# Where q, k and the tails of each batch are turned: crossbar, whole-array or half-array transposes, in a sliding-window attention with a channel mix behind it

## The chip, the cores and the metric

The kernel runs on one core of one Trainium2 chip. The metric is device time in microseconds of one execution; lower is better. A core has TensorE (PE: matmuls, and transposes as matmuls with an identity), VectorE (DVE), ScalarE (ACT), GpSimd (POOL, here an issuer of DMAs that cast fp32 to bf16), SyncE (SP, an issuer of DMAs and of the DMA crossbar's transposes) and 16 DMA engines that all queues share.

## The reference

Eight batches of eight heads, 576 positions, head size 64. Attention looks back over a window of 128 with a linear penalty per head; its output, heads side by side, is the input of a channel mix.

```python
scores = scale * np.matmul(q, k.transpose(0, 1, 3, 2))
rel = pos[:, None] - pos[None, :]
bias = slopes[:, None, None] * (-np.abs(rel))[None]        # slopes = 2 ** -(h + 1)
scores = np.where((rel >= 0) & (rel < 128), scores + bias[None], -1e9)
attn = softmax(scores)                                     # over keys
x = matmul(attn, v).transpose(0, 2, 1, 3).reshape(8, 576, 512)
# channel mix; x_prev is x one position earlier
xk = mu_k * x + (1 - mu_k) * x_prev
xr = mu_r * x + (1 - mu_r) * x_prev
k = np.maximum(xk @ w_k, 0)                                # 512 -> 1024
out = sigmoid(xr @ w_r) * ((k * k) @ w_v)                  # 1024 -> 512
```

## The kernel before

**An order planned on the host.** Each step (a block of matmuls, a copy, a DMA issue) is a node with an estimated length, dependences, the buffers that it takes and frees, and a priority. `Plan.run` plays the nodes through in an event loop and emits the instructions of each engine in the order that comes out; on the chip each engine runs its own list in order, with semaphores between them. `rank` gives an attention step of batch b and head pair g (k = 4b + g) the turn `(k - A[e]) * SLOPE` on engine e; a step of the channel mix has as its turn the sum of the estimated matmul times of the mix before it. The smaller turn goes first when both are ready. `LOADS` is the order of the first loads on POOL's queue: v and V are the two halves of batch 0's v, 2 and 3 the second part of its q and k (heads 0 to 3, 4 to 7), t its tails, K and k the halves of w_k, a, b and c batch 1's q and k, tails and v, R is w_r, W and w are the halves of w_v. Batches 2 to 7 follow as a, b, c.

**Attention, per batch and pair of heads (g = 0 to 3).** q and k are loaded with positions on the partitions and have to be turned so that the head dimension lies there (two heads of 64 rows). The first 512 positions are turned in one of three ways. Batch 0 is special: loaded in two parts, `part` 0 from fp32 stages (L1046, L1049) and `part` 1 by `qk_quad`. `WIDE` batches are loaded head by head with four successive positions in one piece, and are turned by `qk_quad` (L1002: 64x64 blocks). `XB` batches are turned by the DMA crossbar from SP's queue, eight transposes per batch (L467, `flip`). The others are turned by `qk_full`: eight 128x128 transposes into one PSUM bank, one ACT copy of 1024 columns. With `QM` above 0, `qk_some` does it for QM pairs at a time, in 64-row halves: two transposes run in the two halves of the array, into two banks, and four ACT copies of 512 columns (for QM = 2) follow. The last 64 positions (the tails) come as one tile for q and k and are turned by four PE transposes and a DVE copy (`tails`, L856), or for batches in `XTT` by one crossbar transpose (`tail_flip`, L560).

`scores` (L658, K = 64 rows) fills two PSUM pairs, ACT takes exp (L672), DVE multiplies by the mask (L685; batch 0 adds the bias by matmuls, L645, instead). `attend` (L716) multiplies by v with a column of ones behind it, and DVE divides (L722, L727). The output is turned back: by the crossbar for batches in `XO` (6 and 7, L839), otherwise on PE, either whole (`out_t`, L754: five 128x128 transposes, one ACT copy of 576) or, with `OM` above 0, in 64-row halves (`out_some`, L771: ten half-array transposes, two banks, two ACT copies). `shift` makes xk and xr on DVE (L814, L821).

**The channel mix** goes over pairs of batches P, in column ranges of 256, 512 or 384: w_k (L907), relu on ACT (L914), square (L880), then per 128 rows w_r (L925), tanh on ACT (L932), w_v (L941), a product on DVE (L946) and the output's DMA. `order` counts these ranges.

**Buffers.** Four single PSUM banks (`uno`, class p1) are shared by the mix, the transposes and the warm-up matmuls; two pairs (`duo`, p2) serve scores and attend. There are two buffers each for the loaded q and k (cb), v (vs), tails (ts), and crossbar results (qx), and four for turned q and k (qk). Ninety warm-up matmuls (L619) have the last priority and fill PE's free time at the start.

Of the kernel before, what the change touches and what calls it, by code (L numbers as in the profile page):

```python
# [179 lines left out]
def kernel(  # L180
# [12 lines left out]
    nc = tc.nc  # L193

    B, H, S, D = q.shape
    DM = H * D
    DF = moe_w_k.shape[1]
    G = H // 2
    NF = S // 128
# [7 lines left out]
    SM = 128 * NF  # L207
    RELU_SCALE = 0.5 ** 0.5

    PE, ACT, DVE, POOL, SPE, FAB, VIR = "PE", "ACT", "DVE", "POOL", "SP", "FAB", "VIR"  # L210
    NQ, NA, NX, NV, NC = 4, 4, 3, 2, 2
    XB = range(5, B)
    XO = range(6, B)
    X0 = 16
    NWARM = 90
    LOADS = 'v23KtVkabcRWw'
    XD = 6
    OTL = 1.5
    FIN = 384
    RATE = 284.0  # L220
    WIDE = (1,)
    PART_WIDE = True
    QUAD = 0.0565
    RUN = {2: 64 * 284 / 329.0, NF: 128 * 284 / 357.0}
    FLIP = 1.25
    NO = 5
    WAIT = 2.0
    QM = 0
    OM = 1

    def XU(b, g):
        return (DVE,)

    def SQ(order):
        return (DVE,)

    XT0 = (ACT,)
    QK0 = (ACT, DVE)
# [1 line left out]
    FT = (2, 3)  # L240
    KQ = ACT
    VCUT = True
    XTT = range(6, B)
    MMASK = False
    VDEP = 1
    TCOST = 1.5
# [14 lines left out]
    ts_buf = many(2, [128, H, D], BF16, "ts")  # L261
    tt_buf = many(2, [128, G, 3, 64], BF16, "tt")
# [23 lines left out]
    ident = cst.tile([128, 128], BF16, name="ident")  # L286
# [16 lines left out]
    def one(h):  # L303
        return uno[h.idx if h.cls == "p1" else N1 + h.idx]

    def two(h):
        return duo[h.idx]

    plan = Plan(dict(qx=2, xb=2, p2=2, p1=N1, pt=4 - N1, qk=NQ, at=NA, xu=NX, vs=NV, cb=NC, ts=2, tt=2, xt=2, dl=2, dl0=4,
                     xk=2, rl=3, kk=3, rs=4, ot=NO),  # L310
                {}, WAIT)
# [5 lines left out]
    def act_t(n, sb=False):  # L317
        return (n + (112 if sb else 61)) / 1200.0

    def dve_t(n, fast=1):  # L320
        return (n / fast + 66) / 960.0

    AHEAD = 30.0
    A = {PE: 14.25, ACT: 4.00, DVE: 4.50, VIR: 0}
    NBIAS = 4
    XRL = 3.0
    MODE = 0
    EARLY = 0.0
    SLOPE = 4.5

    def rank(prio):

# [9 lines left out]
    def op(e, dur, deps, prio, emit, need=(), free=()):  # L342
        prio = rank(prio)
        return plan.add(e, dur, LAT.get(e, 0.2) if isinstance(e, str) else LAT[e[0]] if len(e) == 1 else 0.22,
                        deps, prio, emit, need, free)

    last = {}

    def virtual(key, holds):
        n = plan.add(VIR, 0.0001, 0.0001, [last.get(key)], (0,), None, holds)  # L350
        last[key] = n
        return n
# [11 lines left out]
    def dma(queue, kb, issue, emit, deps=(), need=(), free=(), lat=(1.0, 0.9)):  # L364
        n = plan.add(queue, issue, 0.0, list(deps) + [last.get(queue)],
                     (len(plan.nodes),), emit, need)
        last[queue] = n
        return fab(queue, kb / RATE, n, lat, free)
# [38 lines left out]
    n_ident = dve_op(0.11, emit_ident, [n_iota], (0, -1))  # L407
# [21 lines left out]
    def issue_t(nd):  # L429
        return 0.53 + 0.00034 * nd  # L430
# [16 lines left out]
    def tail_load(b):  # L447
        h = Hold("ts")
        g = virtual("ts", [h])
        ns = []  # L450
        for i in range(2):
            src = (q, k)[i][b, :, SM:S].rearrange("h p d -> p h d")
            ns.append(dma(POOL, 128 * TCOST, issue_t(512), lambda e, i=i, src=src: nc.gpsimd.dma_start(
                out=ts_buf[h.idx][64 * i:64 * i + 64], in_=src), [g]))
        return h, ns
# [4 lines left out]
    def full_load(b, i, h, g):  # L460
        src = (q, k)[i][b, :, 0:SM].rearrange(
            "h (r p) d -> p h r d" if b in XB else "h (p r) d -> p h r d", p=128)
        return [dma(POOL, 256, issue_t(1024), lambda e, r=r: nc.gpsimd.dma_start(  # L463
# [58 lines left out]
    th, tl, n_w, src1 = {}, {}, {}, {}  # L522
# [31 lines left out]
    cw, ch, cl, xbh, xbl, tth, ttl, ttg = {}, {}, {}, {}, {}, {}, {}, {}  # L554
# [10 lines left out]
    def batch_load(b, what):  # L565
# [7 lines left out]
        elif what == "b":  # L573
            th[b], tl[b] = tail_load(b)
            if b in XB:
                xbh[b] = Hold("qx")
# [9 lines left out]

    for what in LOADS:
        load_step(what)
# [8 lines left out]
    for (c0, n) in DSEG:  # L597
        n_copy[c0] = dve_op(dve_t(n, 4), lambda e, c0=c0, n=n: nc.vector.tensor_copy(
            out=dist[:, c0:c0 + n], in_=dist[:, 0:n]), [n_dist], (0, 1))
    n_sid = [dve_op(0.1, lambda e, h=h: nc.vector.tensor_scalar(  # L600
        out=sid[:, h], in0=ident, scalar1=-(2.0 ** (-(h + 1))) / scale, scalar2=None,
# [6 lines left out]
    def emit_mu(e):  # L608
# [5 lines left out]
        out=mu_sb.rearrange("p i o -> p (i o)"), in_=one(h_mu)[:, 0:2 * NPO]), (), [h_mu])  # L614
# [12 lines left out]
    def copy_any(e, out, in_):  # L627
        (nc.scalar.copy if e == ACT else nc.vector.tensor_copy)(out=out, in_=in_)  # L628
# [213 lines left out]
            res.append(fab(SPE, 1.0 * rows / 128, n, (1.0, 0.9), [hx]))  # L842
        return res

    def tails(b, prio):
        htt = Hold("tt")
        hs = th[b]
        if b in XTT:
            plan.follow(last["tt"], ttg[b])
            last["tt"] = ttg[b]  # L850
            return tth[b], ttl[b]
        hp = Hold("p1")

        def emit(e):
            for g in range(G):
                nc.tensor.transpose(  # L856
                    one(hp).bitcast(BF16)[:, 128 * g:128 * g + 128],
                    ts_buf[hs.idx][:, 2 * g:2 * g + 2].rearrange("p h d -> p (h d)"), ident)

        def emit_c(e):  # L860
            copy_any(e, tt_buf[htt.idx][:, :, 0:2].rearrange("p g t c -> p g (t c)"),
                     one(hp).bitcast(BF16)[:, 0:128 * G].rearrange("p (g w) -> p g w", g=G))

        t = op(PE, 0.0565 * G, list(tl[b]) + [n_ident], prio + (0,), emit, [hp], [hs])
        g = virtual("tt", [htt])
        c = [op(DVE, dve_t(512), [t, g], prio + (0,), emit_c, (), [hp])]
        return htt, c


# [2 lines left out]

    n_hw = 39 + sum(4 if g in FT else 2 for g in range(3)) + 8 * len(XB) + len(XTT) + NJ * len(XO)
    n_split = -n_hw % 8
# [119 lines left out]
    def qk_quad(b, g, nr, buf, deps, prio, c0, hq, take, free):  # L994

        hp = [Hold("p1"), Hold("p1")]

        def emit(e):
            for n in range(2 * nr):
                for hl, r in ((0, 0), (1, 1), (1, 0), (0, 1)):  # L1000
                    rows = slice(64 * r, 64 * r + 64)
                    nc.tensor.transpose(  # L1002
                        one(hp[r]).bitcast(BF16)[64 * hl:64 * hl + 64, 64 * n:64 * n + 64],
                        buf()[rows, n // nr, 2 * g + hl, n % nr], ident[rows, rows])

        t = op(PE, QUAD * 2 * nr, list(deps) + [n_ident], prio + (3,), emit,
               hp + ([hq] if take else []), free)
        t.rows, t.lazy = (64, 64), True
        w = 64 * nr
        ys = [op(QK0 if b == 0 else ACT, {ACT: act_t(2 * w), DVE: dve_t(2 * w)}, [t], prio + (3,),  # L1010
                 lambda e, r=r: copy_any(
            e, qk_buf[hq.idx][:, :, c0 + w * r:c0 + w * r + w].rearrange("p t (c r) -> p t c r", r=nr),
            one(hp[r]).bitcast(BF16)[:, 0:2 * w].rearrange("p (t r c) -> p t c r", t=2, r=nr)),
                 (), [hp[r]]) for r in range(2)]
        return hq, ys
# [6 lines left out]
    for part in range(2):  # L1022
        if part == 1:
            htt, n_tt = tails(0, (0, 0, 1, 0))
        for g in range(G):
            prio = (0, 0, part, g)
# [12 lines left out]
            hp = Hold("p1") if part == 0 else None  # L1039
# [13 lines left out]
            if part:  # L1053
                ys = qk_quad(0, g, 2, lambda: part_buf, cs, prio, 256, hq0[g], False, [])[1]
            else:
                cold = 1.8 if part == 0 and g < 2 else 1.0
                t = op(PE, (0.115 if f32 else 0.0565) * 4 * cold, cs + [n_ident], prio + (3,), emit_t,
                       [hp] + ([hq0[g]] if part == 0 else []))
                ys = [op(QK0, {ACT: act_t(512), DVE: dve_t(512)}, [t], prio + (3,),
                       lambda e, part=part, g=g, hp=hp, f32=f32: copy_any(  # L1060
                    e, qk_buf[hq0[g].idx][:, :, 0:256],
                    one(hp).rearrange("p (t c) -> p t c", t=2)) if f32 else copy_any(
                    e, qk_buf[hq0[g].idx][:, :, 256 * part:256 * part + 256].rearrange(
                        "p t (c r) -> p t c r", r=2),
                    one(hp).bitcast(BF16)[:, 0:512].rearrange("p (t r c) -> p t c r", t=2, r=2)),
                    (), [hp])]
            ha = Hold("at")
            es = []
            for j, (pieces, m0) in enumerate(PART[part]):
# [8 lines left out]
            r, hx = attend(0, g, t0, t1, ha, es + vl[0][0:2] + (vl[0][2:] + blank if part else []),  # L1078
                           prio)
            a, c = out_t(0, g, t0, t1, hx, [r], prio, xh[0], xth[0], late if part == 0 else None)  # L1080
# [31 lines left out]
    for j, (c0, n) in enumerate(MSEG):  # L1112
        n_mcopy.append(op(DVE, dve_t(8 * n, 4), ms + n_mcopy, (2, j),
                          lambda e, c0=c0, n=n: nc.vector.tensor_copy(
            out=mask[:, 0:H, c0:c0 + n], in_=mask[:, 0:H, 0:n])))
# [48 lines left out]
    for b in range(1, B):  # L1164
# [6 lines left out]
        htt, n_tt = tails(b, (0, b, 0, 0))  # L1171
        for g in range(G):
            prio = (0, b, 0, g)
            ha = Hold("at")
            if b in XB:
                hq, y = xbh[b], xbl[b]
# [13 lines left out]
            r, hx = attend(b, g, 0, NJ, ha, [m0, m1] + vl[b] + rs[0:1], prio)  # L1190
# [60 lines left out]
```

The softmax here doesn't subtract the row's maximum and nothing guards it: scores larger than these inputs give would overflow.

## Time and profile before

| | |
|---|---|
| median of 4 runs | 235.41 us (234.73 to 236.2) |
| profiled execution | 236.2 us, its span 234.1 us |
| clock granted to TensorE | 1.00 |
| PE, DVE, ACT, POOL busy | 227.4, 189.4, 160.8, 97.6 us |
| DMA: POOL's queue | 102736 packets, 16.26 MB |
| DMA: SP's and ACT's queues | 26592 packets, 14.50 MB |
| crossbar transposes | 24 of q and k, 10 of outputs, 2 of tails |

The profile is one execution. Busy times overlap between engines. Matmuls are pipelined, so the time shown for one is longer than its share of PE: the distance from start to start tells what a block costs. "L907" is a line of the kernel, and instructions of a helper all have the helper's line; where a wait is listed, the name behind the arrow is what ended it.

### The profile page before, as it was taken

How to read it: one execution, taken by the hardware profiler on the slowest of the kernel's cores; microseconds unless marked ns; L12 is line 12 of the kernel's file. 1: busy time of each engine (PE TensorE's matmuls, PEld its weight loads, DVE VectorE, ACT ScalarE, POOL GpSimd, SP SyncE). 2: the span in 40 equal slices, each digit the busy share in tenths (PEclk: the TensorE clock that was granted, in tenths of full speed). 3: DMA queues.
4: the chain of work that ended last, by engine and by line, in shares of the span. 5: the costliest groups of instructions: out<-in, count | busy, mean ns of one | idle time of the engine just before them, and what ended most of it. 6: DMA issues, size and time to landing. Idle time of an engine off the chain costs nothing.

```text
span 234.1 us, 6268 instructions
## 1 busy us (share of the span) xinstructions
PE 227.4 (97%) x2487; PEld 136.9 (58%) x2487; DVE 189.4 (81%) x427; ACT 160.8 (69%) x292; POOL 97.6 (42%) x124
## 2 busy tenths in 40 slices
PE   7999988999999999999999999999999999999994
PEld 6576866456575765555565755454655744445462
DVE  6577977987897999989989979995869996974242
ACT  3478999659998987984884975947594726326251
POOL 8976673897892694057807854200000000000000
PEclk9999999999999999999999999999999999999999
DMA  6999999999999799679999999996242124121122
GB/s 162 176 174 195 164 174 180 148 201 194 168 137 172 86 143 187 121 108 173 202 137 144 140 186 187 162 111 170 79 101 89 48 48 146 46 90 48 60 74 90
DMA packets 131100, 31.73 MB, mean 136 GB/s; under 512 B 120056, under 2 KB 127232, under 8 KB 131072
## 3 DMA queue, kind: packets, MB, share of 16 engines
q0 software_dynamic: 102736, 16.26, 101.5%
q1 hardware_dynamic: 26592, 14.50, 27.9%
q10 hardware_dynamic: 1744, 0.59, 1.0%
q8 instruction: 19, 0.31, 0.6%
q14 instruction: 9, 0.07, 0.1%
HBM read 33.56 MB, written 9.44 MB: 184 GB/s over the span
## 4 chain that ended last, share of the span: by engine, by line
PE 89%; ACT 5%; DMA 2%; issue 1%; DVE 1%; SPq 0%; DVEq 0%; ACTq 0%
PE uno L941 27%; PE uno L907 26%; PE uno L925 14%; PE duo L716 6%; PE duo L658 6%; PE uno L771 2%; PE uno L1154 2%; ACT at L672 2%; DMA qx<-in_q_dram 2%; PE duo L645 1%; PE uno L619 1%; ACT mask L1088 1%; ACT qk L628 1%; PE uno L1046 1%; PE uno L856 1%
## 5 line engine op out<-in xcount | busy, mean ns | idle before, releaser
L941 PE MATMUL uno<-wv_sb,kk 128*128 128x512 bf16 (+2 forms) x296 | 71.8, 374 | 0.0
L907 PE MATMUL uno<-xk,wk_sb 128*128 128x256 bf16 (+2 forms) x416 | 69.5, 314 | 0.7 <-ACT rl L914 0.4
L672 ACT ACTIVATE at<-duo 128x1024 bf16<-128x1024 f32 (+2 forms) x68 | 65.9, 1005 | 5.8 <-PE duo L658 5.3
L914 ACT ACTIVATE rl<-uno 128x256 bf16<-128x256 f32 (+2 forms) x104 | 47.3, 493 | 20.3 <-PE uno L907 19.1
L907 PEld LDWEIGHTS <-wk_sb 128*128 128x128 bf16 x416 | 38.7, 98 | 22.1 <-issue 0.9
L685 DVE TENSOR_TENSOR at<-at,mask 128x1024 bf16<-128x1024 bf16 x56 | 37.7, 680 | 8.1 <-ACT at L672 7.8
L438 POOL DMA_DIRECT2D vs<-in_v_dram x32 | 28.3, 899 | 33.9 <-PE duo L716 30.4
L941 PEld LDWEIGHTS <-kk 128*128 128x128 bf16 x296 | 26.4, 98 | 26.2
L880 DVE TENSOR_TENSOR kk<-rl 128x256 bf16<-128x256 bf16 (+2 forms) x104 | 33.0, 336 | 9.3 <-ACT rl L914 7.8
L932 ACT ACTIVATE rs<-uno 128x512 bf16<-128x512 f32 x36 | 22.2, 615 | 26.1 <-PE uno L925 23.1
L925 PE MATMUL uno<-wr_sb,xr 128*128 128x512 bf16 x144 | 37.0, 379 | 0.5 <-ACT rl L914 0.5
L946 DVE SCALAR_TENSOR_TENSOR ot<-rs,uno 128x512 f32<-128x512 bf16 (+2 forms) x37 | 24.7, 669 | 12.1 <-PE uno L941 9.7
L821 DVE SCALAR_TENSOR_TENSOR xk<-dl,mu_sb,xt 128x576 bf16<-128x576 bf16 (+1 forms) x32 | 24.8, 781 | 0.4
L716 PEld LDWEIGHTS <-at 128*128 128x128 bf16 x576 | 21.8, 98 | 5.7 <-issue 0.6
L821 DVE SCALAR_TENSOR_TENSOR xr<-dl,mu_sb,xt 128x576 bf16<-128x576 bf16 (+1 forms) x32 | 24.5, 771 | 0.0
L463 POOL DMA_DIRECT2D cb<-in_k_dram x24 | 21.3, 906 | 7.4 <-DMA wv_sb<-in_moe_w_v_dram 3.4
L628 ACT COPY xt<-uno 128x256 bf16<-128x256 bf16 (+1 forms) x48 | 17.1, 405 | 9.0 <-PE uno L771 8.8
L463 POOL DMA_DIRECT2D cb<-in_q_dram x24 | 21.3, 925 | 2.0 <-DMA vs<-in_v_dram 2.0
L925 PEld LDWEIGHTS <-xr 128*128 128x128 bf16 x144 | 13.5, 98 | 14.6 <-issue 0.7
L628 ACT COPY qk<-uno 128x1024 bf16<-128x1024 bf16 (+2 forms) x26 | 18.9, 778 | 3.0 <-PE uno L1049 1.7
L716 PE MATMUL duo<-vs,at 128*128 128x65 bf16 x448 | 19.1, 193 | 0.0
L814 DVE TENSOR_TENSOR dl<-xt 128x576 bf16<-128x576 bf16 (+1 forms) x32 | 13.8, 436 | 4.2 <-ACT xt L628 4.2
(78 smaller groups left out, 209.5 us busy)
## 6 DMA issues: line engine op xcount, KB each, us to landing
out_dram<-ot SPq DMA_DIRECT2D x30, 256.0 KB, 5.1
vs<-in_v_dram POOLq DMA_DIRECT2D x32, 128.0 KB, 7.2
cb<-in_q_dram POOLq DMA_DIRECT2D x24, 128.0 KB, 7.6
cb<-in_k_dram POOLq DMA_DIRECT2D x24, 128.0 KB, 7.5
out_dram<-ot SPq DMA_DIRECT2D x10, 128.0 KB, 1.8
wk_sb<-in_moe_w_k_dram POOLq DMA_DIRECT2D x2, 512.0 KB, 8.3
wv_sb<-in_moe_w_v_dram POOLq DMA_DIRECT2D x2, 512.0 KB, 10.9
qx<-in_k_dram ACTq DMA_DIRECT2D x4, 128.0 KB, 4.8
```

Source lines behind the costliest of these rows:

```text
L438: return dma(POOL, 256, issue_t(1024), lambda e: nc.gpsimd.dma_start(out=vs_buf[h.idx][:, j, :, 0:D], in_=v[b, :, 128 * j:128 * j + 128].r ...
L463: return [dma(POOL, 256, issue_t(1024), lambda e, r=r: nc.gpsimd.dma_start(out=cb_buf[h.idx][:, i, r], in_=src[:, :, r]), [g]) for r in ra ...
L628: (nc.scalar.copy if e == ACT else nc.vector.tensor_copy)(out=out, in_=in_)
L672: lambda e, ah=ah, w=w, hp=hp: nc.scalar.activation(out=ah(), in_=two(hp)[:, :, 0:w], func=AF.Exp, scale=float(scale)), (), [hp])
L685: nc.vector.tensor_tensor(out=a, in0=a, in1=m, op=ALU.mult)
L716: nc.tensor.matmul(a[:, hl, t - t0], lhsT=at[:, lo:lo + 128], rhs=vs[:, u, 2 * g + hl, :] if u < NF else tvb[:, 2 * g + hl], start=(u == u ...
L821: lambda e: nc.vector.scalar_tensor_tensor(out=buf[hk.idx][:, g, e0 + c0:e0 + c1], in0=dls(), scalar=mu[:, g:g + 1], in1=xc(1), op0=ALU.mu ...
L880: nc.vector.tensor_tensor(out=out, in0=in_, in1=in_, op=ALU.mult)
L907: nc.tensor.matmul(one(hp)[:, 0:n], lhsT=wk_sb[:, po, 128 * fo:128 * fo + 128], rhs=xk_buf[hx.idx][:, po, c0:c1], start=(po == 0), stop=(p ...
L914: a = op(ACT, act_t(n), [s], pr, lambda e, hp=hp, hr=hr: nc.scalar.activation(out=rl_buf[hr.idx][:, 0:n], in_=one(hp)[:, 0:n], func=AF.Rel ...
L925: nc.tensor.matmul(one(hp), lhsT=xr_buf[hx.idx][:, po, 128 * c:128 * c + 128], rhs=wr_sb[:, po], start=(po == 0), stop=(po == NPO - 1))
L941: nc.tensor.matmul(one(hv)[:, a:b], lhsT=kk_buf[hk.idx][:, fo, o:o + 128], rhs=wv_sb[:, fo, a:b], start=(fo == 0), stop=(fo == NFO - 1))
```

## The change

Batch 5's q and k leave the crossbar (`XB` from batch 6). Batches 3, 4 and 5 are turned by `qk_some` in pairs of g (`QM` 2), batch 2 joins batch 1 in the head-by-head form (`WIDE`), and the copies of batches 1 and 2 may go to ACT or DVE (`QK1`). Tails of batches 4 and 5 go to the crossbar (`XTT` from 4); batch 0's tails are loaded with four positions in a piece and turned by 16 small matmuls and two DVE copies (`TW`). Outputs of batches 1 to 5 are turned whole, not in halves (`OM` 0). The squares of mix orders 0 to 2 may go to ACT. w_k's first half is loaded before batch 0's second part of q and k, and w_r before batch 1's v. The planner's constants (lengths of quads and runs, turns, wait for 64-row work) change too.

```diff
-    XB = range(5, B)
+    XB = range(6, B)
-    LOADS = 'v23KtVkabcRWw'
-    XD = 6
+    LOADS = 'vK23tVkabRcWw'
+    XD = 4
-    WIDE = (1,)
+    WIDE = (1, 2)
-    QUAD = 0.0565
-    RUN = {2: 64 * 284 / 329.0, NF: 128 * 284 / 357.0}
+    QK1 = (ACT, DVE)
+    TW = (0,)
+    QUAD = 0.040
+    RUN = {2: 64 * 284 / 345.0, NF: 128 * 284 / 390.0}
-    WAIT = 2.0
-    QM = 0
-    OM = 1
+    WAIT = 1.0
+    QM = 2
+    OM = 0
     def SQ(order):
-        return (DVE,)
+        return (DVE, ACT) if order < 3 else (DVE,)
-    XTT = range(6, B)
+    XTT = range(4, B)
-    A = {PE: 14.25, ACT: 4.00, DVE: 4.50, VIR: 0}
+    A = {PE: 7.75, ACT: 4.50, DVE: 4.00, VIR: 0}
-    XRL = 3.0
+    XRL = 4.0
-    SLOPE = 4.5
+    SLOPE = 4.7
@@ tail_load
+        if b in TW:
+            for i in range(2):
+                ns.append(dma(POOL, 104, issue_t(128), lambda e, i=i: nc.gpsimd.dma_start(
+                    out=ts_buf[h.idx].rearrange("p h d -> p (h d)")[:, 256 * i:256 * i + 256],
+                    in_=(q, k)[i][b, :, SM:S].rearrange("h (c r) d -> h c (r d)", r=4)), [g]))
+            return h, ns
@@ tails (the code before is now tails_full, for b not in TW)
+            for n in range(8):
+                for hl in range(2):
+                    nc.tensor.matmul(
+                        one(hp)[64 * hl:64 * hl + 64, 64 * n:64 * n + 64],
+                        lhsT=ts_buf[hs.idx][:, n],
+                        rhs=ident.rearrange("p (g t c) -> p t g c", g=G, t=2)[:, hl],
+                        start=True, stop=True)
+        t = op(PE, 0.03 * 16, list(tl[b]) + [n_ident], prio + (0,), emit, [hp], [hs])
+        c = [op(DVE, dve_t(256), [t, g], prio + (0,), lambda e, i=i: copy_any(
+            e, tt_buf[htt.idx][:, :, i].rearrange("p g (c r) -> p g c r", r=4),
+            one(hp)[:, 256 * i:256 * i + 256].rearrange("p (r g c) -> p g c r", r=4, g=G)),
+                (), [hp]) for i in range(2)]
@@ qk_quad
-        ys = [op(QK0 if b == 0 else ACT, {ACT: act_t(2 * w), DVE: dve_t(2 * w)}, [t], prio + (3,),
+        ys = [op(QK0 if b == 0 else QK1, {ACT: act_t(2 * w), DVE: dve_t(2 * w)}, [t], prio + (3,),
```

More of the change, by code (lines that the diff above doesn't have):

```diff
@@ L843, in out_flip, with tails_full @@
         return res
[L845 to L851, printed above, removed]
+    def tails_full(b, prio, htt, hs):
         hp = Hold("p1")
@@ L866, in tails, with emit @@
         c = [op(DVE, dve_t(512), [t, g], prio + (0,), emit_c, (), [hp])]
+        return htt, c
+    def tails(b, prio):
+        htt = Hold("tt")
+        hs = th[b]
+        if b in XTT:
+            plan.follow(last["tt"], ttg[b])
+            last["tt"] = ttg[b]
+            return tth[b], ttl[b]
+        if b not in TW:
+            return tails_full(b, prio, htt, hs)
+        hp = Hold("p1")
+        def emit(e):
+            for n in range(8):
[6 more added lines that the diff above has]
+        t = op(PE, 0.03 * 16, list(tl[b]) + [n_ident], prio + (0,), emit, [hp], [hs])
+        g = virtual("tt", [htt])
+        c = [op(DVE, dve_t(256), [t, g], prio + (0,), lambda e, i=i: copy_any(
+            e, tt_buf[htt.idx][:, :, i].rearrange("p g (c r) -> p g c r", r=4),
+            one(hp)[:, 256 * i:256 * i + 256].rearrange("p (r g c) -> p g c r", r=4, g=G)),
+                (), [hp]) for i in range(2)]
         return htt, c
```

## The prediction

> **What bounds the kernel now.** I read the page first, its busy times and the chain that ended last:
>
> ```profile
> ## 1 busy us (share of the span) xinstructions
> PE 227.4 (97%) x2487; PEld 136.9 (58%) x2487; DVE 189.4 (81%) x427; ACT 160.8 (69%) x292; POOL 97.6 (42%) x124
> ...
> PE 89%; ACT 5%; DMA 2%; issue 1%; DVE 1%; SPq 0%; DVEq 0%; ACTq 0%
> ```
>
> TensorE (PE) carries the end. But "busy" counts the warm-up matmuls of L619, which compute nothing and are planned only where PE has nothing else. So I read busy time by stretches (columns after the stretch: its length, then busy us and count for PE, weight load, DVE, ACT, POOL):
>
> ```profile
> 0.00:10.00 10.00, 8.49 (x60) 6.07 (x61) 5.93 (x37) 4.07 (x5) 8.40 (x17) 1.00 1.21 166
> 10.00:20.00 10.00, 10.00 (x189) 6.92 (x188) 8.06 (x26) 7.01 (x15) 7.46 (x11) 1.00 1.73 181
> 20.00:30.00 10.00, 9.60 (x198) 7.41 (x197) 8.62 (x27) 9.73 (x28) 7.12 (x9) 1.00 2.10 171
> 30.00:40.00 10.00, 8.62 (x166) 6.51 (x165) 7.64 (x20) 9.73 (x20) 5.32 (x7) 1.00 1.62 185
> 40.00:50.00 10.00, 10.00 (x116) 5.51 (x115) 9.71 (x19) 6.42 (x11) 8.84 (x11) 1.00 2.22 164
> ```
>
> From 40 us on PE never idles; from 20 to 40 us it does, and there ACT is full (9.73 of 10). Next, PE's own waits from 43 to 231 us, and POOL's longest over the run:
>
> ```profile
> PE uno L907 <- ACT qk L628: 0.2, 1, 0.2
> ```
> ```profile
> POOL vs L438 <- PE duo L716: 30.4, 4, 11.7
> ```
>
> PE waits 0.2 us in 188, so there the time is the sum of PE's work. POOL stands idle 30 us until PE's attention frees a buffer: from 74 us on loads are early, not late. Last, PE in order of time (start, busy, then what). A block's real cost is the next block's start minus its own:
>
> ```profile
> 23.78 0.45 PE L619 MATMUL uno<-warm 128*128 128x128 bf16 x5
> ...
> 29.51 1.00 PE L1002 MATMUL uno<-ident,cb 64*64 64x64 bf16 x64
> 30.68 0.27 PE L856 MATMUL uno<-ident,ts 128*128 128x128 bf16 x2 [0.17 <-ACT qk L628]
> 31.40 0.27 PE L856 MATMUL uno<-ident,ts 128*128 128x128 bf16 x2 [0.45 <-issue]
> 31.51 1.47 PE L907 MATMUL uno<-xk,wk_sb 128*128 128x256 bf16 x12
> 32.91 0.56 PE L658 MATMUL duo<-qk 64*128 64x256 bf16 x8
> ...
> 33.46 0.45 PE L1002 MATMUL uno<-ident,cb 64*64 64x64 bf16 x32
> 33.84 1.05 PE L907 MATMUL uno<-xk,wk_sb 128*128 128x256 bf16 x8
> ...
> 38.49 1.02 PE L925 MATMUL uno<-wr_sb,xr 128*128 128x512 bf16 x4 [0.48 <-ACT rl L914]
> ```
>
> **PE time lost at the start.** Warm-up blocks, start to next start: 0.27, 0.45, 0.22, 0.68, 0.12, 0.28, 0.67 from 10 to 18 us, 2.69 in all; 0.29 and 0.45 at 23.78 and 24.84. From 26 to 38.5 us blocks are stretched against the same block unhindered: L1002 x32 takes 0.80 at 26.18 and 0.38 at 33.46 (+0.42); the x64 at 29.51 1.17 against 0.76 (+0.41); L856 0.83 against 0.23 at 53.46 (+0.60); scores at 34.81 0.86 against 0.55 (+0.31); L907 at 35.67 1.63 against 1.40 (+0.23); attend at 37.30 1.19 against 0.55 (+0.64). That is 2.61, with the two warm-ups 3.35 us lost from 20 to 40 us. This and the 2.69 are all that a better start can give; the first 5 us (first load lands at 5.12) stay.
>
> **Part by part.** *R before c.* PE's first L925 block starts at 38.49, and wr_sb lands at 35.13. It now goes ahead of batch 1's five v loads, which land from 28.03 to 33.43: 5.4 us earlier, 29.7. Four L925 blocks of 0.86 (3.44 us) then exist for the gap; two need only part 0's xr, done at 20.7. Batch 1's v lands 1.7 later (wr's own spacing, 33.43 to 35.13), at 35.1; its first reader starts at 37.30, so 2.2 us cover it; beyond that each late us would delay attention. POOL's queue behind it (W, w, batch 2) moves by nothing.
>
> *ACT relief there.* Batch 1's output copies go from two (10.1/24 + 9.1/24 = 0.80 us) to one of 576 columns, 0.62 between the 512 (0.57) and 1024 (0.99) rows: 0.18 x 4 = 0.7. Its eight qk copies (0.57) may go to DVE; half of them is 2.3. Squares of orders 0 to 2 may go to ACT and take some back; DVE is at 8.6 and 7.6 of 10 there. From these two I take 2.0 of the 3.35 as recovered. Bounds: 3.35 gained, or 1.0 lost if attention comes later.
>
> *K before 2 and 3.* K spans 2.6 us of landings (12.21 to 14.83), so part 1's q and k land at 13.3 and 14.8 instead of 10.72 and 12.21. The first part-1 transposes (12.34) are pushed 1.0 us; the third (16.82) has cover. The first L907 (19.68) waited not for wk (landed 14.83) but for the fourth xk, which DVE ended at 19.10 after four part-1 qk copies of about 0.4 on DVE; moved behind it, they let L907 replace warm-ups. Taken: 0.5 gained; bounds 1.5 gained, 1.0 lost. The batch-0 tail load with longer pieces (its two loads hold 1.4 us of landings now) frees at most that and is covered.
>
> *PE work.* Output transposes of batches 1 to 5: I count 12 of the 20 half-array blocks next to other 64-row work, 0.155 each (79.75 to 79.90), and 8 alone, 0.25 plus 0.10 on the block before: 4.7 us. Full ones cost 5 x 0.056 = 0.28 (six take 0.34 at 24.50): 5.6, so +0.9. q and k: batch 2 from 4 x 0.45 (73.98 to 74.42) to 4 x 0.38: -0.3. Batches 3 and 4: eight blocks, 3.6 us, become four pairs of 16 double steps at 0.031 (the 0.155 for five): 0.50 each, 0.70 alone, 2.4 taken: -1.2. Batch 5 had no PE transposes: two pairs, +1.2. Tails of batches 4 and 5 leave PE: -0.46; batch 0's become 16 small matmuls for 0.32: +0.15 (0 to +0.5). Sum +0.3, bounds -0.5 to +1.2.
>
> [...]
>
> *Copies.* Batches 3 to 5: four ACT copies of 512 per pair, 2.3 us, against two of 1024, 2.0; in return 20 output copies shorter by 0.18 (3.6 us). ACT is at 5.7 to 9.5 of 10 after 40 us and feeds a full PE; cost 0, and what it costs if the cover is gone is the second rival.
>
> *Crossbar.* Eight transposes of 1.3 us leave SP's queue (92 to 102 us) and two tail ones come; output writes behind them go sooner. Nobody on PE waits there: 0. Batch 5's cb buffer is now held until PE has read it, and batch 7's loads (first issue 128.37) want it; batch 4's transposes are done by about 97, 9 us before batch 6's loads want that buffer at 106.33, so 0 too.
>
> *Turns at the end.* New SLOPE and A put step 31's ACT turn at 26.5 x 4.7 = 124.6 instead of 27 x 4.5 = 121.5, DVE's at 126.9 instead of 119.3, so attention of batch 7 may end 3 to 7.6 us later (now 187.5). XD leaves the last shifts' turn where it was (145.7 against 146.2). Batch 6's mix covers it from 191.9 to 208.3; 0 taken, and the third rival prices it.
>
> **Sum:** -2.0 - 0.5 + 0.3 = -2.2 us. The profiled execution took 236.2 (span 234.1 and 2.1 around it), so 234.0; it was the slowest of four, 0.8 over the median, so I give **233.2** against 235.41. A difference under 0.5% (1.2 us) is about what a measurement of this kernel cannot tell from none.
>
> **Rivals.** *One: the start stays as it is*, because ACT's exps and masks set it and the freed loads only wait: 0.3 of PE work added, little gained, 234.8 to 236. For it: ACT's 9.73; against it: PE lost 3.35 us there with no L925 allowed before wr. *Two: PSUM banks.* A pair takes two of the four uno banks until four ACT copies are done (2.3 us each bank against 1.0 for one bank). The channel mix needs banks of the same four, and the one wait after 43 us is PE on such a copy. If each of six pairs stops PE for one more copy and its latency, 0.9, it costs 5.4: 233.2 + 5.4 = 238.6; above 0.4 us a pair it decides the sign. Against it: half-array outputs hold two banks 20 times now, with no wait. *Three: batch 7 late.* Its last xk is done at 207.2 and L907 wants it at 208.3. A slip of 7.6, less the 3.7 us that DVE can save there by doing its four dl and xk first (5.0 of the 9.7 us from 197.5), less the 1.1, leaves PE 2.8 us idle near 208: 236.0; it decides beyond a slip of 7.
>
> **Chances.** Forecast 0.58 (231 to 234.2), start unchanged 0.17, banks 0.14, batch 7 late 0.11. The forecast counts as faster, and a few of the other cases are too; the range reaches from a start fully mended (233.2 - 2.4, rounded to 230.8) to a bank cost of about 0.65 a pair (237.2). Faster 0.60, same 0.18, slower 0.22.
>
> **What will show it.** Right: no stretched L1002 or L856 between 26 and 38 us, L925 before 36, first L907 before 19.7, ACT below 9.7 there; PE gapless after 40; PE's last block some 2 us before 228.2. Wrong: PE waits named ACT qk in batches 3 to 5, L907 waiting for DVE xk near 208, or the warm-up count between 10 and 26 us grown.

## The result and the profile after

The changed kernel takes 234.26 us (median of 41 runs, 233.46 to 236.9) against 235.27 us for the kernel before on the same occasions (62 runs). The ratio is 0.9955, with a 95% interval of 0.9945 to 0.9965: 1.0 us, or 0.45%, gained where 2.2 were forecast. The profiled execution took 234.04 us, its span 232.3.

Busy time by stretches of the changed kernel (columns as before: length, then PE, weight load, DVE, ACT, POOL):

```profile
10.00:20.00 10.00, 9.94 (x191) 6.50 (x190) 8.01 (x26) 7.35 (x17) 7.58 (x11) 1.00 1.79 176
20.00:30.00 10.00, 9.70 (x203) 7.72 (x204) 7.98 (x23) 10.00 (x31) 6.31 (x8) 1.00 1.65 187
30.00:40.00 10.00, 9.21 (x177) 7.02 (x173) 8.89 (x20) 9.95 (x22) 5.32 (x8) 1.00 1.68 182
40.00:50.00 10.00, 10.00 (x195) 6.18 (x192) 9.94 (x19) 9.00 (x17) 6.66 (x8) 1.00 1.87 194
```

PE's hole from 20 to 40 us is smaller, not gone (busy 18.91 of 20 us against 18.22), and ACT, which was to be relieved, is fuller (10.00 and 9.95 against 9.73 twice). PE's waits in the changed kernel from 18 to 43 us; from 43 to 231 us the list is empty:

```profile
PE uno L955 <- DVE qk L636: 0.7, 1, 0.7
PE uno L937 <- ACT qk L636: 0.3, 1, 0.3
```

The same place in order of time (PE; L955 is the w_r block, L925 before; L1032 the quads of 64x64 blocks, L1002 before; L937 is the w_k block, L907 before; L636 is the copy out of PSUM, L628 before):

```profile
26.43 1.96 PE L937 MATMUL uno<-xk,wk_sb 128*128 128x256 bf16 x16 [0.30 <-ACT qk L636]
28.23 0.33 PE L762 MATMUL uno<-ident,xu 128*128 128x128 bf16 x3
28.39 0.39 PE L858 MATMUL uno<-ident,ts 128*128 128x128 bf16 x4
...
30.16 0.89 PE L1032 MATMUL uno<-ident,cb 64*64 64x64 bf16 x64
31.77 1.02 PE L955 MATMUL uno<-wr_sb,xr 128*128 128x512 bf16 x4 [0.71 <-DVE qk L636]
...
33.41 1.02 PE L955 MATMUL uno<-wr_sb,xr 128*128 128x512 bf16 x4
```

The stretched L856 is gone (now L858, 28.39 to 28.66), and w_r blocks run 6.7 us sooner (31.77 against 38.49). The two quads in a row are still stretched (1.61 us from 30.16 to 31.77, against the 0.76 unhindered of the prediction): they (x64) fill all four uno banks, and the w_r block needs one, so it waits until a q and k copy has emptied it. That is the second rival's mechanism, in batch 1 at the start, where the prediction did not look for it.

A balance of PE, from the starts of all its blocks. Each block's distance to the next start is split into three parts: its unhindered cost (one value per form for all three traces, such as 0.216 us for a matmul of 512 columns, 0.28 for a quad, 0.47 for the half-array transposes of a pair), 0.1 us at each change between 128-row and 64-row work or between two forms of 64-row work, and the rest, which is lost. In the changed kernel 28 matmuls of 512 columns take 6.04 us from 190.82 to the next start; four of them take 0.96 us before scores (95.13) and 0.87 before a w_v block (103.76); the last matmul of the scores takes 0.12 before a quad (30.04), 0.13 before a w_r block (103.63) and 0.03 before a pair's half-array transposes (96.51). Warm-up blocks count as lost.

| us on PE | before, profiled (236.2) | before, another execution (234.84) | changed (234.04) |
|---|---|---|---|
| unhindered work | 206.2 | 206.2 | 207.0 |
| changes of rows | 10.3 | 10.3 | 9.5 |
| lost or warm-up, 0 to 10 us | 5.5 | 4.8 | 4.7 |
| 10 to 20 us | 2.8 | 2.5 | 2.9 |
| 20 to 43 us | 3.8 | 3.5 | 2.6 |
| after 43 us | 1.4 | 1.4 | 1.4 |
| sum | 230.0 | 228.8 | 228.1 |

The middle column is the run before_held_r_early below, whose engines have the order of the kernel before (only w_r's load is moved). It shows that the profiled execution of before lost about 1 us to a late start (its first load landed at 5.12 us; here at 4.25, in the changed kernel at 4.34). Against the middle column the change does this: work +0.8, changes of rows -0.8, 0 to 10 us -0.1, 10 to 20 us +0.4, 20 to 43 us -1.0, after 43 us nothing, in all -0.7. So work and changes of rows cancel, and PE's gain lies between 20 and 43 us. The 0.5 us of stalls after 43 us that an expectation below names as a difference between the two traces is not there in this count. Another 0.2 lies outside the span: the median time is 1.98 us longer than the span for the kernel before and 1.78 for the changed one; why is not known.

### The profile page after: what moved, and what is told of

Read it like the earlier page. It is cut to its first block, busy times and chain, and to the rows that moved or that the text cites. A ratio compares the mean times of both kernels' runs of the same rounds, so it can differ in the third digit from the quotient of the medians.

```text
span 232.3 us, 6483 instructions
## 1 busy us (share of the span) xinstructions
PE 226.2 (97%) x2615; PEld 138.6 (60%) x2615; DVE 188.5 (81%) x416; ACT 166.1 (72%) x302; POOL 93.5 (40%) x120
## 4 chain that ended last, share of the span: by engine, by line
PE 91%; ACT 3%; DMA 2%; issue 1%; SPq 1%; DVE 1%; DVEq 0%
PE uno L971 27%; PE uno L937 26%; PE uno L955 13%; PE duo L666 7%; PE duo L724 7%; PE uno L762 3%; DMA qx<-in_q_dram 2%; PE duo L653 1%; PE uno L779 1%; PE uno L627 1%; PE uno L724 1%; ACT qk L636 1%; PE uno L1032 1%; ACT rl L944 1%; SPq L490 1%
## 5 line engine op out<-in xcount | busy, mean ns | idle before, releaser
L937 PE MATMUL uno<-xk,wk_sb 128*128 128x256 bf16 (+2 forms) x416 | 69.4, 314 | 0.3 <-ACT qk L636 0.3
L680 ACT ACTIVATE at<-duo 128x1024 bf16<-128x1024 f32 (+2 forms) x68 | 64.9, 998 | 4.3 <-PE duo L666 4.0
L944 ACT ACTIVATE rl<-uno 128x256 bf16<-128x256 f32 (+2 forms) x104 | 47.9, 487 | 21.0 <-PE uno L937 19.1
L937 PEld LDWEIGHTS <-wk_sb 128*128 128x128 bf16 x416 | 39.2, 98 | 22.6 <-issue 0.7
L910 DVE TENSOR_TENSOR kk<-rl 128x256 bf16<-128x256 bf16 (+2 forms) x91 | 29.9, 344 | 11.1 <-ACT rl L944 9.7
L955 PE MATMUL uno<-wr_sb,xr 128*128 128x512 bf16 x144 | 37.0, 379 | 0.8 <-DVE qk L636 0.7
L724 PEld LDWEIGHTS <-at 128*128 128x128 bf16 x576 | 21.8, 98 | 5.6 <-issue 1.2
L636 ACT COPY qk<-uno 128x512 bf16<-128x512 bf16 (+1 forms) x43 | 22.7, 602 | 1.9 <-PE uno L1079 1.0
L955 PEld LDWEIGHTS <-xr 128*128 128x128 bf16 x144 | 13.2, 98 | 14.4 <-issue 0.7
L636 ACT COPY xt<-uno 128x576 bf16<-128x576 bf16 (+2 forms) x28 | 16.1, 584 | 5.1 <-PE uno L762 5.1
L724 PE MATMUL duo<-vs,at 128*128 128x65 bf16 x448 | 19.1, 194 | 0.0
L471 POOL DMA_DIRECT2D cb<-in_k_dram x20 | 17.8, 908 | 2.5 <-DMA vs<-in_v_dram 1.0
L471 POOL DMA_DIRECT2D cb<-in_q_dram x20 | 17.7, 917 | 1.4 <-PE duo L724 1.2
## 6 DMA issues: line engine op xcount, KB each, us to landing
cb<-in_q_dram POOLq DMA_DIRECT2D x4, 256.0 KB, 10.2
cb<-in_k_dram POOLq DMA_DIRECT2D x4, 256.0 KB, 10.3
```

Source lines behind the costliest of these rows:

```text
L680: lambda e, ah=ah, w=w, hp=hp: nc.scalar.activation(out=ah(), in_=two(hp)[:, :, 0:w], func=AF.Exp, scale=float(scale)), (), [hp])
L724: nc.tensor.matmul(a[:, hl, t - t0], lhsT=at[:, lo:lo + 128], rhs=vs[:, u, 2 * g + hl, :] if u < NF else tvb[:, 2 * g + hl], start=(u == u ...
L910: nc.vector.tensor_tensor(out=out, in0=in_, in1=in_, op=ALU.mult)
L937: nc.tensor.matmul(one(hp)[:, 0:n], lhsT=wk_sb[:, po, 128 * fo:128 * fo + 128], rhs=xk_buf[hx.idx][:, po, c0:c1], start=(po == 0), stop=(p ...
L944: a = op(ACT, act_t(n), [s], pr, lambda e, hp=hp, hr=hr: nc.scalar.activation(out=rl_buf[hr.idx][:, 0:n], in_=one(hp)[:, 0:n], func=AF.Rel ...
L955: nc.tensor.matmul(one(hp), lhsT=xr_buf[hx.idx][:, po, 128 * c:128 * c + 128], rhs=wr_sb[:, po], start=(po == 0), stop=(po == NPO - 1))
```

## The experiments

Two kinds. In the first a constant is put back and the planner makes a new order. In the second the planned order is held, and one thing is moved in it. Each was timed in five rounds beside the kernel before; times are medians, to be compared with 234.26 (changed) and about 235.3 (before).

**One part, planned anew.** Edits: in the kernel before `LOADS = 'vK23tVkabRcWw'` (before_new_loads); in the changed kernel `LOADS = 'v23KtVkabcRWw'` (after_old_loads); `QK1 = (ACT,)` and all squares `(DVE,)` (after_no_act_relief); A, SLOPE, XD, XRL and WAIT of before (after_old_turns).

> The kernel before with the new order of the first loads alone (w_k's first half before batch 0's second part of q and k, w_r before batch 1's v). Start theory: w_r lands near 30 instead of 35 us, a w_r block (L925) runs before 36 us, PE loses 0.5 to 1.0 us less between 20 and 43 us, so 234.3 to 234.8 against 235.27. Rival, the gain comes from PE's work or from the new turns after 43 us: no change, 235.1 to 235.4.

> The changed kernel with the old order of the first loads. Start theory: w_r blocks cannot run before 35 us again, 0.5 to 1.0 us are lost, 234.8 to 235.3 against 234.26. Rival (work or turns): 234.1 to 234.4.

> The changed kernel with the q and k copies of batches 1 and 2 on ACT alone and all squares on DVE. Start theory: ACT is full from 20 to 40 us in both kernels, and the copies on DVE save it about 2 us there; without them PE loses 0.3 to 0.8 us more between 20 and 43 us: 234.6 to 235.1. Rival, ACT gets as much work back in squares as it gives away in copies: 234.1 to 234.4.

> The changed kernel with the planner's turns of before (A, SLOPE, XD, XRL, WAIT). Start theory: PE is gapless after 43 us with either set, so the turns bring nothing: 234.1 to 234.5. Rival, the turns save the 0.8 us of switches between 128-row and 64-row work and the 0.5 us of stalls after 43 us that the two traces differ by: 235.0 to 235.6.

Measured: 236.88, 238.78, 236.68 and 237.87 us. No part could be taken out, and none added to the kernel before, without a loss of 1.6 to 4.5 us, more than the whole change gains. That fits neither theory: parts worth 2.4 to 4.5 us each do not add up to 1.0. The same balance of the four traces says where the losses lie: from 20 to 43 us PE loses 3.7, 2.9, 3.0 and 2.3 us (3.5 to 3.8 before, 2.6 changed), but after 43 us 2.1, 5.5, 4.0 and 4.4, where both kernels lose 1.4. PE's longest wait after 43 us with the old loads:

```profile
PE uno L937 <- ACT rl L944: 1.1, 1, 1.1
```

So most of the loss with the old loads and with the old turns is not at the start, where the start theory looked. In before_new_loads the w_r blocks do run sooner (32.83 us instead of 38.49), and PE's loss there stays 3.7. So either the parts need each other or a new plan costs something by itself. The control:

```diff
-    A = {PE: 7.75, ACT: 4.50, DVE: 4.00, VIR: 0}
+    A = {PE: 8.00, ACT: 4.50, DVE: 4.00, VIR: 0}
```

> The changed kernel with PE's turn 8.00 instead of 7.75: nothing is removed or added, only another order comes out of the same planner. It prices what any new plan costs. If the order is not fragile: 234.1 to 234.6, and the 1.6 to 4.5 us that taking back the loads, the engines or the turns cost are theirs. Rival, a plan fitted to the chip loses by any re-planning: 235.0 to 237.5, and those costs cannot be put down to the parts.

Measured: 235.60 us, ratio to before 1.0011 (0.9991 to 1.0031). A plan that differs only in what the planner made of this constant gives the whole gain back. The start is the same (2.6 us lost from 20 to 43); after 43 us PE loses 2.9 instead of 1.4. Its longest waits there, from PE's list for 20 to 240 us (L724 is attend, L680 the exp):

```profile
PE duo L724 <- ACT at L680: 0.7, 1, 0.7
...
PE uno L955 <- ACT qk L636: 0.6, 1, 0.6
```

The second is a w_r block behind a q and k copy again, now at 66.5 us. So the four results above cannot be read as prices of the parts. One control gives the price of one other plan, 1.3 us, and not the most that another plan may cost; the losses of 4.0 to 5.5 us after 43 us may be order as well. For the load of w_r and for the engines the runs with the order held settle it. For the old turns (+3.6) there is none: turns and plan are the same thing there.

**One thing moved, order held.** The added code shifts the lines of the kernels by 3 to 5 (in the changed one L959 is the w_r block, L940 w_k, L639 the copy, L947 relu, L966 tanh; in before_held_r_early L929 is the w_r block and L917 relu). First w_r:

```diff
+        r = seq.pop(at("R"))
+        seq.insert(at("c", 1) + 1, r)      # behind batch 1's v, on POOL alone
```

> The changed kernel with every engine's order held as planned, and one thing moved: POOL issues w_r behind batch 1's v again. Start theory: the two w_r blocks at 31.8 and 33.4 us wait until w_r lands near 35 us, PE loses 2.5 to 3.4 us at that place and gets none of it back: 236.8 to 237.7. Rival, ACT sets the pace between 20 and 40 us and PE would have waited there anyway: 234.3 to 235.5.

Measured: 238.42 us, 4.2 more. PE stands before the first w_r block as long as its data is missing:

```profile
34.20 1.89 PE L959 MATMUL uno<-wr_sb,xr 128*128 128x512 bf16 x4 [3.29 <-DMA wr_sb<-in_moe_w_r_dram]
```

w_r landed at 34.16 us. The wait is 3.29 us where the changed kernel waits 0.71, so 2.6 more, at the lower end of the theory. The rest of the 4.2 is not in the wait: this block took 1.83 us to the next start instead of 0.95, and the scores and the second w_r block behind it were slow too. From 34 to 38 us the clock granted to PE was 0.55 and 0.60, which is 1.8 and 1.6 us at half clock if the rest was at full (columns: length, PE busy, granted clock, DMA share, GB/s):

```profile
32.00:34.00 2.00, 0.00 (x0) 1.00 1.26 207
34.00:36.00 2.00, 1.79 (x4) 0.55 1.20 196
36.00:38.00 2.00, 2.00 (x17) 0.60 1.25 205
38.00:40.00 2.00, 2.00 (x32) 1.00 1.42 197
```

From the first w_r block to the end of the second, PE took 3.96 us (34.20 to 38.16) instead of 2.50 (31.77 to 34.27): some 1.4 us for the clock. All six executions of this run show a mean granted clock of 0.986 to 0.992. The theory priced the wait alone, and the time lies above its range. The mirror image is the kernel before with w_r early and its order held:

> The kernel before with every engine's order held and w_r issued ahead of batch 1's v on POOL, as the changed kernel has it. PE's order has its first w_r block behind two attend blocks at 38.5 us, 3.4 us after w_r lands, so an early w_r alone brings nothing and v lands 1.7 us later under cover: 235.0 to 235.6. Rival, w_r's landing was what held PE at 35 to 38 us: 232.5 to 234.5.

Measured: 235.02 us, ratio 0.9995 (0.9978 to 1.0013): no change, as the start theory has it. w_r landed at 30.16, and the first w_r block waited for something else:

```profile
37.33 1.02 PE L929 MATMUL uno<-wr_sb,xr 128*128 128x512 bf16 x3 [0.48 <-ACT rl L917]
```

So the early load and PE's order belong together: the load alone is worth nothing, and the order without it costs 4.2 us (2.6 of waiting and some 1.4 of half clock).

Then the engines: `n.eng = ACT` for the q and k copies of batches 1 and 2, `n.eng = DVE` for the squares.

> The changed kernel with the planned order held, and the engines given back as before: the four q and k copies of batches 1 and 2 that DVE makes go to ACT, the thirteen squares that ACT makes go to DVE. Start theory (copies on DVE relieve ACT): PE loses 0.3 to 0.8 us more between 25 and 40 us, 234.6 to 235.1. Rival, ACT got back more in squares than it gave away: 233.8 to 234.3.

Measured: 235.97 us, 1.7 more. The start theory has the place right, but the loss is more than twice as large as it expected. PE loses 4.5 us instead of 2.6 from 20 to 43 us, and the waits carry the name of ACT's copies:

```profile
PE uno L959 <- ACT qk L639: 1.3, 2, 1.0
PE uno L940 <- ACT rs L966: 0.4, 1, 0.4
PE uno L940 <- ACT rl L947: 0.4, 1, 0.4
```

ACT does less in this run (thirteen squares fewer, four copies more; 8.98 and 9.22 us busy from 20 to 30 and 30 to 40 us instead of 10.00 and 9.95), yet PE waits longer, and for ACT's copies of the banks: ACT's busy share over these stretches does not tell how long PE waits. Between 30 and 35 us, where the copies stand, ACT is nearly as full as before (4.91 of 5 against 5.00). Copies and squares were moved together here, so their shares are not told apart.

Two attempts to do better than the change. The copy that PE waits for goes ahead of an xk product and a square on DVE:

> The changed kernel with the planned order held, but on DVE the copy that PE waits for at 31 us (batch 1, third pair, first bank) goes ahead of the xk product and the square in front of it. If PSUM banks held by that copy cause the 0.7 us wait of the first w_r block: the wait shrinks to 0.2 to 0.3 us and the time to 233.7 to 234.0. Rival, the block behind waits as long for ACT's copies: 234.2 to 234.4.

Measured: 234.43 us, not told apart from 234.26. Both w_r blocks now wait, for 0.4 us each (0.71 and nothing before); the second for ACT:

```profile
31.28 1.02 PE L959 MATMUL uno<-wr_sb,xr 128*128 128x512 bf16 x4 [0.38 <-DVE qk L639]
...
33.27 1.02 PE L959 MATMUL uno<-wr_sb,xr 128*128 128x512 bf16 x4 [0.41 <-ACT qk L639]
```

The loss from 20 to 43 us is the same, 2.56 us. The rival was right. So ACT was given less as well:

```diff
+        for n in seq:
+            if n.tag and n.tag[:2] == ("sq", 0):
+                n.eng = DVE
```

> The changed kernel with the planned order held, the copy on DVE put first as in the run before, and the four squares of the first mix range that ACT makes between 25 and 29.5 us given to DVE. If ACT's load (10.0 of 10 us busy there) sets the copies that free the banks for the w_r blocks, its copies come up to 1.3 us sooner and PE loses 0.5 to 0.9 us less between 25 and 34 us: 233.4 to 233.9. Rival, DVE (8 to 9 of 10) is then late with xk, and the stall only changes its name: 234.2 to 235.0.

Measured: 234.57 us, again no better, and again the rival's case: the w_r blocks wait 0.49 and 0.30 us, together as long as in the run before, and PE stands 0.43 us before a w_k block:

```profile
30.41 0.60 PE L940 MATMUL uno<-xk,wk_sb 128*128 128x256 bf16 x4 [0.43 <-ACT rl L947]
```

The trace is of an execution 0.9 us above the median, whose loads before 20 us landed late, so its start is compared by these waits and not by its sum.

No version tried beats the changed kernel.

**PE's work.** Outputs in halves again (`OM = 1`):

> The changed kernel with the outputs of batches 1 to 5 turned in halves again (OM = 1). By the two traces whole outputs cost PE 2.5 us more of transposes; halves cost switches of 0.2 us where no other 64-row work stands beside them, 8 of 20 before. Work theory: transposes and switches of PE fall by about 0.9 us; a new plan costs 1 to 1.5 as the run with another plan did: 234.3 to 235.0. Rival: two banks for each output stop the mix as well, 235.5 to 237.

Measured: 235.51 us. In its trace the transposes fall by 2.5 us and the changes of rows rise by 1.6 (11.1 against 9.5), the -0.9 of the sum; but after 43 us PE loses 3.4 instead of 1.4. 235.51 is what the other plan costs too, so the price of the halves' two banks can't be told from that of a new plan.

Batch 5 on the crossbar again (`XB = range(5, B)`):

> The changed kernel with batch 5's q and k turned by the crossbar again. By the unit of 0.5 us a pair PE gets rid of 1.0 us and two switches of 0.2; nobody waits for the eight crossbar transposes; a new plan costs 1 to 1.5: 234.0 to 234.9. Rival: the transposes crowd SP's queue and the DMA engines and delay loads and output writes, 235.5 or more.

Measured: 238.07 us, 3.8 more, and not for the reason that its rival named: no load is late, and PE runs ahead of the changed kernel until 203 us. Then the mix of batch 7 finds no xk:

```profile
207.68 0.48 PE L937 MATMUL uno<-xk,wk_sb 128*128 128x384 bf16 x2 [1.21 <-DVE ot L976]
208.41 0.32 PE L937 MATMUL uno<-xk,wk_sb 128*128 128x384 bf16 x1 [0.24 <-DVE xk L829]
210.24 7.77 PE L937 MATMUL uno<-xk,wk_sb 128*128 128x384 bf16 x29 [1.51 <-DVE xk L829]
```

Attention of batch 7 ends at 190.7 instead of 187.3, its outputs come back from the crossbar at 201.5, its last xk starts at 209.4. This is the third rival's place and mechanism. PE waits only 0.3 us in all from 100 to 200 us, so attention is late because PE's planned order has it late, and not because PE stood still for the crossbar. Whether the eight crossbar transposes made the planner order it so, or any new plan would have, stays open; a kernel with the order held was not tried here. Nor is the median the price of the wait alone: three of the six executions had a mean granted clock of 1.000 and took 237.43 to 237.73 us, three had 0.983 to 0.993 and took 238.41 to 239.5. The trace is of the slowest; its clock is looked at in the last section.

## Why the prediction was half right

*What bounds the kernel*: right for the two kernels and for the runs with the order held: PE's work and its holes from 20 to 43 us make their time. In the runs planned anew PE also loses 2.1 to 5.5 us after 43 us, and in after_crossbar_b5 it waits near 208.

*R before c and ACT relief, -2.0*: the mechanism holds in part, and the term was mis-sized: -1.0. The failed step is the way in which it was bounded: the loss was compared with the w_r work that became possible (3.44 us) and with ACT's busy time, and no bank was counted. Two of the four w_r blocks came into the gap, and both stand behind quads whose copies hold all four banks. The relief of 3.0 us on ACT did not come: by 43 us DVE makes three of batch 1's eight copies, ACT makes nine squares (3.6 us in its rows) and is at 10.00. after_held_engines shows that the exchange pays all the same, for DVE now makes copies that free banks. That early w_r blocks alone do not close the hole is shown by before_new_loads (w_r at 32.83 us, 3.7 lost) and after_held_engines (w_r at 33.19, 4.5 lost); how the -1.0 divides between load and engines is not shown.

*K before 2 and 3, -0.5*: nothing gained. Warm-ups fill 2.8 us from 10 to 20 us, against 2.7 and 2.4 in the two traces of the order of before. The first w_k block came at 19.19 instead of 19.68, but the first load had come 0.8 us sooner in that execution; with the first load as early, the order of before has it at 18.74.

*PE work, +0.3*: 0.0 (work +0.8, changes of rows -0.8), inside its bounds. Outputs: +2.5 of transposes, of which the forecast's count of lone halves gives back 1.6: +0.9 as said. q and k: -1.4 of transposes, a pair costing 0.47 and a change of rows behind it, 0.56 from start to start where 0.60 was taken; tails -0.25 against -0.3. The other changes of rows add 0.8.

*Copies, 0*: right for batches 3 to 5 (no wait in PE's list after 43 us). *Turns, 0*: the place that the forecast named stayed covered (attention of batch 7 ended at 187.3, no wait near 208). What it left out is that turns make the whole order: after_other_plan shows that a quarter of a step in one turn costs 1.5 us after 43 us, in the time 1.3. The cover was an order fitted to this work, not a reserve. *Crossbar, 0*: not shown; see above.

*From profile to median*: the forecast took off 0.8 us because its execution was the slowest of four. The later runs put that execution 0.9 above the median of before, so this step held.

*Rivals*: the unchanged start did not come, nor batch 7 late; the banks did, in two or three blocks of the start instead of six pairs later. The forecast's range, 230.8 to 237.2, also holds the time of before, so that the result lies inside it says little; the forecast gain was twice the real one.

## What to carry to other kernels

Where the order of every engine is planned, a part of a change can't be priced by putting its constant back: plan variants that differ in nothing else as controls (one, as here, gives a price but no bound), and hold the order to move one thing. When a load is brought forward to fill a hole, count the buffers (here PSUM banks) that the new work needs at that moment and who empties them, not only the busy share of the engine that seemed to be the limit. Here a load and the order that uses it paid only together. When a wait is priced, read the granted clock behind it as well: here 0.55 and 0.60 in the 4 us behind a wait of 3.29.

## What the runs showed of the hardware

In after_held_r_late one pause of 3.29 us was followed by some 3.4 us at half clock (granted 0.55 and 0.60, rows above). In the profiled execution of after_crossbar_b5, after pauses of 1.2, 0.2 and 1.5 us near 208 us, PE was granted 0.50 of its clock from 210 to 216, and 0.83 and 0.96 in the 2 us before and behind, some 6.8 us at half clock in all (columns as above):

```profile
206.00:208.00 2.00, 0.79 (x5) 1.00 0.34 131
208.00:210.00 2.00, 0.49 (x3) 0.83 0.35 135
210.00:212.00 2.00, 1.76 (x6) 0.50 0.00 0
212.00:214.00 2.00, 2.00 (x7) 0.50 0.00 0
214.00:216.00 2.00, 2.00 (x8) 0.50 0.00 0
216.00:218.00 2.00, 2.00 (x13) 0.96 0.00 0
```

So in this execution a wait of 3 us cost about 6: the 32 w_k matmuls from 207.68 took 10.2 us to the next start, where 5.2 is their unhindered cost (28 of them take 4.55 from 207.87 in the changed kernel), and 1.2 had gone before them. Three of the six executions of this kernel, with a mean granted clock of 1.000, show no such loss. What length of pause brings it is not shown. The prediction's third rival left this out, and priced only the wait.
